# Gate and up products on separate halves of TensorE's rows, and both block turns in the down phase, in a fused long convolution and SwiGLU layer

## The chip, the cores and the metric

The kernel runs on one core of a Trainium2 chip. The metric is the device time of one execution in microseconds (us), the median of several runs. The core has a matrix engine (TensorE, PE in the profile; its weight loads are listed apart as PEld), a vector engine (VectorE, DVE), an activation engine (ScalarE, ACT), a general engine (GpSimd, POOL) and a sync engine (SyncE, SP) whose queue issues nearly all DMAs here. TensorE multiplies a stationary operand of up to 128 rows by 128 columns with a moving operand of up to 512 columns, and writes to PSUM. PSUM is used as four buffers of two banks, 512 float32 values per partition in each bank. SBUF is the working memory of 128 partitions.

## What is computed

A sequence of S = 2048 tokens with D = 576 features goes through two residual halves. The first is a gated long convolution: its causal convolution runs along the sequence, as products of spectra. The second is a feed-forward layer with F = 4608 hidden columns. Both have a layer norm and a modulation by a row that a condition vector gives.

```python
x = A_q
sa, ca, ga, sb, cb, gb = ...                     # six rows of silu(c) @ w_mod
h = layernorm(x) * (1 + ca) + sa
x = x + ga * conv_part(h, A_k, A_v, ...)         # q * (long convolution of (shifted k * v))
h = layernorm(x) * (1 + cb) + sb
gate = h @ w1                                    # 576 -> 4608
up = h @ w3                                      # 576 -> 4608
x = x + gb * ((silu(gate) * up) @ w2)            # 4608 -> 576
```

All inputs are bfloat16; sums are kept in float32.

## The kernel before

The convolution works in eight blocks of 256 tokens (B), the feed-forward layer in four row blocks of 512 tokens (RB), so that a row block holds two convolution blocks. `run` computes block 0 of the convolution first (`first_block`). Then a first stage runs 24 of the 36 hidden tiles of 128 columns for tokens 0 to 255, while the convolution of block 1 is worked off beside it (`conv_second`). Then `row_blocks` runs r = 0 to 3. Row block 0 begins with the two chunks whose weights are still in place, then alternates between the three chunks that are new (all 512 tokens) and the four that need only tokens 256 to 511.

A row block has an up phase (`stream`) and a down phase (`down`). While they run, the convolution of the two blocks of the next row block (`conv`) is worked off a step at a time. It is a Python generator; after each item `advance` pulls so many of its steps as the spent time allows, so its instructions stand between the products on every engine's queue. `outcome` ends a block's convolution: real parts of the accumulated spectrum z, inverse transform, the residual, the second layer norm into `h2row`.

**The turn.** The products need the normed rows with the features on partitions. `turn_all` does that for a block of 256 tokens: ten transposes of 128 columns (five for each of two token groups) into one PSUM buffer, then five evictions on ACT (`turned`, line 601), which also apply scale and shift per feature (`cbcol`, `sbcol`). 576 features are four full tiles of 128 and a rest of 64. So that the rest can serve gate and up at once, its 64 features are written twice into the row (columns 512 to 575 and 576 to 639), and land on partitions 0 to 63 and 64 to 127 of the fifth tile. The turned rows lie in `h2T`, two buffers used in turn by row blocks. The first block is turned by `turn_split` and `turned_split`, on ACT and DVE side by side. The later of a row block's two blocks is turned in the down phase of the row block before (line 985), the earlier one within the convolution, between the residual and the norm of the later (line 856).

**The up phase.** Hidden columns come in nine chunks of four tiles (FC = 4). `load_w13` brings a chunk's columns of w1 and w3 into one of two buffers `wst`, by four DMAs (lines 871 and 872): for each matrix 512 rows as four tiles on 128 partitions (512 KB), and the last 64 rows on partitions 0 to 63 for w1, 64 to 127 for w3 (64 KB). A buffer is loaded again as soon as the products that read it are through. An item is one PSUM buffer: gate in one bank, up in the other, 512 columns each (one hidden tile for 512 tokens, or two for 256). It takes eight full products (`full`, line 916) per hidden tile, and two products of 64 rows for the rest (`rest`, line 927). The latter use different halves of TensorE's rows and run side by side. Items are taken in pairs, or in fours in the last row block: the full products of the early ones, the rests of the early and of the late ones together, then the full products of the late ones. Then `hide` takes silu(gate) and up out of PSUM on ACT and multiplies them on DVE into `h3`.

**The down phase.** For each half h of the 576 output columns, nine chunks of w2 are multiplied (line 979), 16 products of 288 columns for a chunk, four token groups accumulating in two PSUM buffers (four in the last half of all).

Of the kernel before, what the change touches and what calls it, by code (L numbers as in the profile page):

```python
# [9 lines left out]
BF16 = mybir.dt.bfloat16  # L10
F32 = mybir.dt.float32
# [4 lines left out]
P = 128  # L16
S = 2048
D = 576
# [5 lines left out]
RB = 512  # L24
NRB = S // RB
# [9 lines left out]
EPS = 1e-5  # L35

# [7 lines left out]
class _Kernel:  # L44
# [28 lines left out]
    def setup(self):  # L73
# [12 lines left out]
        self.h2T = [const.tile([P, 5, RB], BF16, name=f"h2T{i}") for i in range(2)]  # L86
        self.h2row = const.tile([P, 2, 640], BF16, name="h2row")
# [5 lines left out]
        self.cbcol = const.tile([P, 5], F32, name="cbcol")  # L93
        self.sbcol = const.tile([P, 5], F32, name="sbcol")
# [23 lines left out]
        nc.gpsimd.memset(self.h2T[0][:, 0, :], 0.0)  # L118
# [117 lines left out]
    def mod_columns(self):  # L236
# [13 lines left out]
        nc.scalar.activation(self.cbcol[:], ps[:, 0, 0:5], ACT.Copy, bias=1.0)  # L250
        nc.scalar.copy(self.sbcol[:], ps[:, 1, 0:5])
# [298 lines left out]
    def residual(self, s, y):  # L550
        nc = self.nc
        x1, hg = self.xo[s], self.hg[s]
        nc.vector.tensor_mul(hg[:], hg[:], y[:])
        nc.vector.tensor_add(x1[:], x1[:], hg[:])

    def normed(self, s, cc, m, r):

        row, x1 = self.h2row, self.xo[s]
        self.center(row[:, cc, 0:D], x1[:, cc, :], m, r)
        self.center(row[:, cc, D:640], x1[:, cc, 512:D], m, r)  # L560

    def normed_act(self, s, r, b):
        row, x1 = self.h2row, self.xo[s]
# [5 lines left out]
    def turn(self, pt, cc):  # L569
        for ct in range(5):  # L570
            self.nc.tensor.transpose(pt[:, cc, ct * P:(ct + 1) * P],  # L571
                                     self.h2row[:, cc, ct * P:(ct + 1) * P], self.ident[:])

    def turn_split(self, cc):

        pt = [self.ps((P, 2, 1024), BF16) for _ in range(2)]
        for ct in range(5):
            self.nc.tensor.transpose(pt[ct // 3][:, 0, ct % 3 * P:(ct % 3 + 1) * P],
                                     self.h2row[:, cc, ct * P:(ct + 1) * P], self.ident[:])
        return pt  # L580

    def turned_split(self, pt, cc):
        hT = self.h2T[0]
        for ct in range(5):
            dst, src = hT[:, ct, cc * P:(cc + 1) * P], pt[ct // 3][:, 0, ct % 3 * P:(ct % 3 + 1) * P]
            if ct > 2:
                self.nc.vector.tensor_scalar(dst, src, self.cbcol[:, ct:ct + 1], self.sbcol[:, ct:ct + 1],
                                             op0=ALU.mult, op1=ALU.add)
            else:
                self.nc.scalar.activation(dst, src, ACT.Identity, bias=self.sbcol[:, ct:ct + 1],  # L590
                                          scale=self.cbcol[:, ct:ct + 1])

    def turned(self, s, pt, c0, n):

        nc = self.nc
        hT = self.h2T[(s // 2) % 2]
        t = 2 * (s % 2) + c0
        for ct in range(5):
            dst = hT[:, ct, t * P:(t + n) * P].rearrange("p (c t) -> p c t", c=n)
            src = pt[:, c0:c0 + n, ct * P:(ct + 1) * P]  # L600
            nc.scalar.activation(dst, src, ACT.Identity, bias=self.sbcol[:, ct:ct + 1],  # L601
                                 scale=self.cbcol[:, ct:ct + 1])
# [25 lines left out]
    def first_block(self):  # L628
# [18 lines left out]
        self.warm(3, self.h2T[0][:, 0, :])  # L647
# [3 lines left out]
        self.warm(4, self.h2T[0][:, 0, :])  # L651
# [84 lines left out]
    def outcome(self, s, fill, waits, between=None, quick=False):  # L736


        def steps():
# [3 lines left out]
            y = self.lnp.tile([P, 2, D], BF16, name="y", tag="y")  # L743
# [25 lines left out]

    def turn_all(self, s):  # L770

        pt = self.ps((P, 2, 1024), BF16)
        for cc in range(2):
            self.turn(pt, cc)
        self.turned(s, pt, 0, 2)
# [20 lines left out]
    def conv(self, s0):  # L796
# [59 lines left out]
        yield from self.outcome(s1, ahead, (5.0, 4.5, 5.0, 0.0), lambda: self.turn_all(s0))  # L856
# [7 lines left out]
    def load_w13(self, fc):  # L864
# [5 lines left out]
        for i, w in enumerate((self.w1, self.w3)):  # L870
            nc.sync.dma_start(t[:, 5 * i:5 * i + 4, :], w[0:512, cols].rearrange("(a p) f -> p a f", p=P))
            nc.sync.dma_start(t[64 * i:64 * i + 64, 4, :], w[512:D, cols])
# [12 lines left out]
    def stream(self, r, jobs, rate, size):  # L885

        nc = self.nc
        hT = self.h2T[r % 2]
        items = []
        for job in jobs:
            m = RB // (job[2] - job[1])
            items += [(job, fi, m) for fi in range(0, FC, m)]
        gus, ws = {}, {}

        def load(job):
# [7 lines left out]
            ws[job[0:3]] = w  # L907


        def full(k, first):  # L910
            (fc, t0, t1, _, _), fi, m = items[k]
            w, n = ws[fc, t0, t1], t1 - t0
            for a in range(m):
                for i in range(2):
                    for ct in range(4):
                        nc.tensor.matmul(gus[k][:, i, a * n:(a + 1) * n],  # L916
                                         w[:, 5 * i + ct, (fi + a) * P:(fi + a + 1) * P], hT[:, ct, t0:t1],
                                         start=(first and ct == 0 and a == 0),
                                         stop=(not first and ct == 3 and a == m - 1))

        def rest(k, first):
            (fc, t0, t1, _, _), fi, m = items[k]
            w, n = ws[fc, t0, t1], t1 - t0
            for a in range(m):
                for i in range(2):
                    rows = slice(64 * i, 64 * i + 64)
                    nc.tensor.matmul(gus[k][:, i, a * n:(a + 1) * n],  # L927
                                     w[rows, 4, (fi + a) * P:(fi + a + 1) * P], hT[rows, 4, t0:t1],
                                     start=(first and a == 0), stop=(not first and a == m - 1))

        def hide(k):
            (fc, t0, t1, _, _), fi, m = items[k]
            sg = self.hp.tile([P, RB], BF16, name="sg", tag="sg")
            nc.scalar.activation(sg[:], gus[k][:, 0, :], ACT.Silu)  # L934
            u = self.hp.tile([P, RB], BF16, name="u", tag="u")
            nc.scalar.copy(u[:], gus[k][:, 1, :])  # L936
            f = fc * FC + fi
            nc.vector.tensor_mul(self.h3[:, f:f + m, t0:t1], sg[:].rearrange("p (a t) -> p a t", a=m),  # L938
                                 u[:].rearrange("p (a t) -> p a t", a=m))
            del gus[k]  # L940
            self.advance(rate * 2.05)

        def begin(k):
            if items[k][1] == 0:
                load(items[k][0])
            gus[k] = self.ps()
        for k in range(0, len(items), size):
            early, late = range(k, k + size // 2), range(k + size // 2, k + size)
            for m in early:
                begin(m)  # L950
                full(m, True)
            for m in early:
                rest(m, False)
            for m in late:
                begin(m)
                rest(m, True)
            for m in early:
                hide(m)
            for m in late:
                full(m, False)  # L960
                hide(m)

    def down(self, r, rate):
        nc = self.nc
        for h in range(2):
# [4 lines left out]
            for f0 in range(0, NF, W2C):  # L970
# [11 lines left out]
                if h == 1 and f0 // W2C == 5 and r + 1 < NRB:  # L982

                    self.end()
                    self.turn_all(2 * r + 3)
                if (f0 // W2C) % 4 == 3:
# [118 lines left out]
```

## Time and profile before

| What | us |
|---|---|
| median of 3 runs | 523.21 (521.06 to 523.32) |
| profiled execution, its own time | 520.12 |
| span of that profile (first to last instruction) | 518.3 |
| mean granted TensorE clock | 0.992 |
| PE busy | 499.9 (96% of the span), 3362 products |
| PEld busy | 293.8 (57%) |
| DVE busy | 341.0 (66%) |
| ACT busy | 293.3 (57%) |
| POOL busy | 54.9 (11%) |
| full products of the up phase, line 916 | 267.4 busy, x1344 |
| 64-row products, line 927 | 43.2 busy, x336 |
| down products, line 979 | 145.6 busy, x1152 |
| DMA queue of SP | 107.21 MB, 64.3% of 16 engines |

The page lists each engine's busy time, then a chain of waits: the work that ended last, followed back from the end. Only time on that chain sets the span. The timeline lists one engine's instructions in order, merged into groups: start, length to the end of the last one, the group and its count. A group's length runs past the start of the next one by the depth of the pipeline, so distances between starts are what counts. Views of stretches give each engine's busy time between two moments, and in the last three columns the granted clock, the share of time in which the 16 DMA engines were busy, and the GB/s that they moved.

In time the program falls into these parts: block 0 of the convolution to about 33 us; the first stage to 70.7; row block 0 to 171.4; row block 1 to 291.0; row block 2 to 407.3; row block 3 to the end.

### The profile page before, as it was taken

To read this page: it belongs to the slowest core of one execution; us is meant where nothing else is said; L and a number is where in the kernel's file an instruction comes from. 1 tells how busy PE (TensorE), PEld (TensorE's weight loads), DVE (VectorE), ACT (ScalarE), POOL (GpSimd) and SP (SyncE) were. 2 spreads that over 40 slices of the span, in tenths; PEclk is the share of its full clock that TensorE was granted. 3 is DMA by queue.
4 is the path that set the end of the run, shared out by engine and by line. 5 is a ranking of instruction groups with operands and counts; after the bars stand their busy time and mean duration, and the time that the engine had idled before them with its cause. 6 is when DMAs were issued, how large, how long until landed. Compare 5 with 4: busy or idle time off the path is not lost.

```text
span 518.3 us, 8731 instructions
## 1 busy us (share of the span) xinstructions
PE 499.9 (96%) x3362; PEld 293.8 (57%) x3362; DVE 341.0 (66%) x515; ACT 293.3 (57%) x581; POOL 54.9 (11%) x109
## 2 busy tenths in 40 slices
PE   7999988999999999999998999999999999999997
PEld 3666765555788444444676543434588544444775
DVE  8898996999995355896999995389661212222012
ACT  6668469668543469759561465876816446445000
POOL 3205001204021001202002000120101000000000
PEclk9999889999999999999999999999999999999999
DMA  8959629757679953547999894554455453450462
GB/s 269 313 178 332 201 89 321 275 183 250 197 208 348 330 176 107 188 158 275 363 365 352 318 284 150 165 178 156 152 143 145 147 173 119 161 169 10 118 179 70
DMA packets 102205, 107.77 MB, mean 208 GB/s; under 512 B 5075, under 2 KB 94228, under 8 KB 102164
## 3 DMA queue, kind: packets, MB, share of 16 engines
q1 hardware_dynamic: 102142, 107.21, 64.3%
q8 instruction: 26, 0.43, 0.3%
q14 instruction: 15, 0.12, 0.1%
q10 hardware_dynamic: 22, 0.01, 0.0%
HBM read 96.00 MB, written 11.21 MB: 207 GB/s over the span
## 4 chain that ended last, share of the span: by engine, by line
PE 84%; DMA 8%; ACT 4%; DVE 2%; issue 1%; POOL 1%; DVEq 0%
PE ps L916 46%; PE ps L979 25%; PE ps L927 7%; DMA wst<-in_B_w_dram 5%; DMA w2t<-in_B_w_dram 3%; PE ps L313 2%; PE ps L539 2%; PE ps L364 1%; PE ps L299 1%; ACT junk L440 1%; PE ps L571 1%; PE ps L219 0%; PE ps L626 0%; ACT sg L934 0%; DMA shk_raw<-in_A_shift_k_dram 0%
## 5 line engine op out<-in xcount | busy, mean ns | idle before, releaser
L916 PE MATMUL ps<-h2T,wst 128*128 128x512 bf16 (+1 forms) x1344 | 267.4, 351 | 5.9 <-DMA wst<-in_B_w_dram 3.0
L916 PEld LDWEIGHTS <-wst 128*128 128x128 bf16 x1344 | 128.1, 98 | 128.6 <-issue 19.7
L934 ACT ACTIVATE sg<-ps 128x512 bf16<-128x512 f32 x144 | 86.6, 601 | 117.0 <-PE ps L927 73.9
L979 PE MATMUL ps<-w2t,h 128*128 128x288 bf16 x1152 | 145.6, 286 | 3.1 <-DMA w2t<-in_B_w_dram 2.3
L979 PEld LDWEIGHTS <-h 128*128 128x128 bf16 x1152 | 112.2, 98 | 32.5 <-issue 4.0
L938 DVE TENSOR_TENSOR h<-sg,u 128x512 bf16<-128x512 bf16 x144 | 60.5, 422 | 96.6 <-ACT u L936 96.6
L936 ACT CAST u<-ps 128x512 bf16<-128x512 f32 x144 | 84.5, 587 | 0.2 <-DVE h L938 0.2
L410 DVE TENSOR_TENSOR p<-X,V 128x3456 bf16<-128x3456 bf16 x28 | 54.7, 1953 | 5.1 <-DMA X<-Xd 4.9
L412 DVE TENSOR_TENSOR z<-z,p 128x3456 bf16<-128x3456 bf16 x28 | 54.7, 1954 | 0.2
L997 DVE TENSOR_TENSOR og<-ps,gbrow 128x288 bf16<-128x288 f32 x32 | 13.2, 450 | 48.9 <-PE ps L979 48.9
L927 PE MATMUL ps<-h2T,wst 64*128 64x512 bf16 (+1 forms) x336 | 43.2, 355 | 0.4 <-ACT kT L366 0.4
L440 ACT ACTIVATE junk<-x 128x576 bf16<-128x576 bf16 x54 | 37.5, 695 | 0.5
L601 ACT ACTIVATE h2T<-ps,sbcol,cbcol 128x256 bf16<-128x256 bf16 x35 | 16.7, 569 | 24.8 <-PE ps L571 24.8
L927 PEld LDWEIGHTS <-wst 64*128 64x128 bf16 x336 | 11.6, 95 | 28.1 <-issue 24.1
L455 POOL TENSOR_SCALAR l2m<-l2s 128x2 f32<-128x2 f32 x6 | 8.9, 1476 | 153.3 <-ACT junk L440 153.3
L334 DVE TENSOR_TENSOR kvt<-kh,shk 128x1152 bf16<-128x1152 bf16 x24 | 18.1, 753 | 7.4 <-DMA kh<-in_A_k_dram 7.2
L455 POOL TENSOR_SCALAR l1m<-l1s 128x2 f32<-128x2 f32 x7 | 6.5, 929 | 139.4 <-ACT junk L440 139.4
L566 ACT ACTIVATE h2row<-x,l2n,l2r 128x576 bf16<-128x576 bf16 (+1 forms) x24 | 13.7, 642 | 12.5 <-POOL l2n L460 12.4
L335 DVE TENSOR_TENSOR kv<-kv,kvt 128x1152 bf16<-128x1152 bf16 x24 | 18.1, 753 | 0.3
L315 ACT CAST X<-ps 128x576 bf16<-128x576 f32 x24 | 15.5, 658 | 0.0
L405 DVE TENSOR_TENSOR z<-X,V 128x3456 bf16<-128x3456 bf16 x7 | 13.7, 1953 | 2.5 <-DMA X<-Xd 2.5
L745 ACT CAST y<-ps 128x576 bf16<-128x576 f32 x14 | 8.4, 651 | 10.2 <-PE ps L539 10.2
(137 smaller groups left out, 356.3 us busy)
## 6 DMA issues: line engine op xcount, KB each, us to landing
wst<-in_B_w_dram SPq DMA_DIRECT2D x80, 512.0 KB, 4.5
w2t<-in_B_w_dram SPq DMA_DIRECT2D x72, 288.0 KB, 3.2
X<-Xd SPq DMA_DIRECT2D x8, 864.0 KB, 5.8
Xd<-X SPq DMA_DIRECT2D x6, 864.0 KB, 6.4
wst<-in_B_w_dram SPq DMA_DIRECT2D x80, 64.0 KB, 2.2
kh<-in_A_k_dram SPq DMA_DIRECT2D x7, 720.0 KB, 6.9
Vd<-V SPq DMA_DIRECT2D x4, 864.0 KB, 6.3
V<-Vd SPq DMA_DIRECT2D x4, 864.0 KB, 5.0
```

The source lines that it names most:

```text
L334: nc.vector.tensor_mul(tmp[:], kh[:, 3 - j:5 - j, :], tap(j))
L335: nc.vector.tensor_add(kv[:], kv[:], tmp[:])
L410: nc.vector.tensor_mul(p[:], X[:], V[:])
L412: nc.vector.tensor_add(z[:], z[:], p[:])
L440: self.nc.scalar.activation(junk[:], src[:, i, :], func, accum_out=out[:, col:col + 1])
L601: nc.scalar.activation(dst, src, ACT.Identity, bias=self.sbcol[:, ct:ct + 1], scale=self.cbcol[:, ct:ct + 1])
L916: nc.tensor.matmul(gus[k][:, i, a * n:(a + 1) * n], w[:, 5 * i + ct, (fi + a) * P:(fi + a + 1) * P], hT[:, ct, t0:t1], start=(first and ct ...
L927: nc.tensor.matmul(gus[k][:, i, a * n:(a + 1) * n], w[rows, 4, (fi + a) * P:(fi + a + 1) * P], hT[rows, 4, t0:t1], start=(first and a == 0 ...
L934: nc.scalar.activation(sg[:], gus[k][:, 0, :], ACT.Silu)
L936: nc.scalar.copy(u[:], gus[k][:, 1, :])
L938: nc.vector.tensor_mul(self.h3[:, f:f + m, t0:t1], sg[:].rearrange("p (a t) -> p a t", a=m), u[:].rearrange("p (a t) -> p a t", a=m))
L979: nc.tensor.matmul(acc[t], self.h3[:, f0 + f, t * P:(t + 1) * P], w[:, f, :], start=(f0 + f == 0), stop=(f0 + f == NF - 1))
```

## The change

The contraction over 576 features is cut into nine pieces of 64 (NK). All gate products run on TensorE's rows 0 to 63 and all up products on rows 64 to 127, each pair at once. A hidden tile of 512 tokens takes 18 products of 64 rows where it took eight of 128 and two of 64. `h2T` holds nine turned tiles; tile j has features 64j to 64j + 63 on its lower half and the next 64 on its upper half, so that with tile j gate uses piece j and up piece j + 1. Pairs run in the order FIRST_J = (0, 5, 1, 6, 2, 7, 3, 8, 4). There is no pairing of items any more, one follows the other.

w1's chunk lies on partitions 0 to 63 of `wst` and w3's on 64 to 127, in nine pieces each, so `load_w13` issues two DMAs of 576 KB, to 64 partitions each, in place of four.

Tile j = 8 takes columns 512 to 639 of the normed row, whose last 64 are a copy of columns 512 to 575 as before; the up product meets that copy with the first 64 rows of w3. So up takes its last piece where the reference has its first; this changes no instruction's kind or size.

```diff
-            nc.sync.dma_start(t[:, 5 * i:5 * i + 4, :], w[0:512, cols].rearrange("(a p) f -> p a f", p=P))
-            nc.sync.dma_start(t[64 * i:64 * i + 64, 4, :], w[512:D, cols])
+            nc.sync.dma_start(t[64 * i:64 * i + 64, :, :], w[:, cols].rearrange("(a p) f -> p a f", p=64))
...
+        def products(gu, w, fi, m, t0, t1):
+            n = t1 - t0
             for a in range(m):
...
+                cols = slice((fi + a) * P, (fi + a + 1) * P)
+                for i, j in enumerate(FIRST_J):
+                    for half in range(2):
+                        rows = slice(64 * half, 64 * half + 64)
+                        nc.tensor.matmul(gu[:, half, a * n:(a + 1) * n], w[rows, (j + half) % NK, cols],
+                                         self.h2T[rows, j, t0:t1], start=(i == 0 and a == 0),
+                                         stop=(i == NK - 1 and a == m - 1))
...
+        for job in jobs:
+            fc, t0, t1 = job[0:3]
+            w, m = load(job), RB // (t1 - t0)
+            for fi in range(0, FC, m):
+                gu = self.ps()
+                products(gu, w, fi, m, t0, t1)
+                hide(gu, fc * FC + fi, m, t0, t1)
+                self.advance(rate * 2.05)
```

A turn now has nine transposes per token group (18 for a block) into two PSUM buffers, and nine evictions. Both turns for the next row block stand in the down phase, the earlier block's after the fourth chunk of the first half. There are two buffers of `h2row` and one of `h2T` (there were one and two). The per-feature scale and shift come as nine columns (`cscol`); every second is put together by two small copies on POOL that move 64 partitions to the other half.

```diff
+    def turn_all(self, s):
+
+        pts = [self.ps((P, 2, 1024), BF16) for _ in range(2)]
+        at = lambda j: slice(j % 5 * P, (j % 5 + 1) * P)
+        t = B * (s % 2)
+        for i, pt in enumerate(pts):
+            js = range(5 * i, min(5 * i + 5, NK))
+            for j in js:
+                for cc in range(2):
+                    self.turn(s, cc, j, pt[:, cc, at(j)])
+            for j in js:
+                self.turned(j, self.h2T[:, j, t:t + B].rearrange("p (c t) -> p c t", c=2), pt[:, :, at(j)])
...
+                if h == 0 and f0 // W2C == 3 and r + 1 < NRB:
+                    self.turn_all(2 * r + 2)
...
-        yield from self.outcome(s1, ahead, (5.0, 4.5, 5.0, 0.0), lambda: self.turn_all(s0))
+        yield from self.outcome(s1, ahead, (5.0, 4.5, 5.0, 0.0))
...
+        nc.scalar.activation(cs[:, 0, 0:10:2], ps[:, 0, 0:5], ACT.Copy, bias=1.0)
+        nc.scalar.copy(cs[:, 1, 0:10:2], ps[:, 1, 0:5])
+        nc.gpsimd.tensor_copy(cs[0:64, :, 1:9:2], cs[64:P, :, 0:8:2])
+        nc.gpsimd.tensor_copy(cs[64:P, :, 1:9:2], cs[0:64, :, 2:10:2])
```

In `turned_split` the first block's nine tiles per token group go five to ACT and four to DVE (three and two before), in the order FIRST_J. The output `y` of the inverse transform no longer has a tile of its own but is written into two rows of z that are free by then.

```diff
-            y = self.lnp.tile([P, 2, D], BF16, name="y", tag="y")
+            z = self.accs[s]
+            y = z[:, 2:6:3, :] if s < SPLIT else z[:, 4:6, :]
```

## The prediction

> **What bounds the kernel now.** I read the page's chain of waits first, then TensorE's (PE's) timeline, the chain cut into pieces, and last the stretches that show the DMA engines.
>
> ```profile
> PE 84%; DMA 8%; ACT 4%; DVE 2%; issue 1%; POOL 1%; DVEq 0%
> ```
>
> TensorE sets the end: 84% of the chain. Its timeline, in the second and the last row block (start, length, group):
>
> ```profile
> 213.18 3.63 PE L916 MATMUL ps<-h2T,wst 128*128 128x512 bf16 x16
> 216.74 0.60 PE L927 MATMUL ps<-h2T,wst 64*128 64x512 bf16 x4
> 217.28 3.63 PE L916 MATMUL ps<-h2T,wst 128*128 128x512 bf16 x16
> ...
> 427.75 7.08 PE L916 MATMUL ps<-h2T,wst 128*128 128x512 bf16 x32
> 434.76 1.04 PE L927 MATMUL ps<-h2T,wst 64*128 64x512 bf16 x8
> 435.73 7.08 PE L916 MATMUL ps<-h2T,wst 128*128 128x512 bf16 x32
> ```
>
> Two items take 217.28 - 213.18 = 4.10 us, four take 435.73 - 427.75 = 7.98 us, each with one excursion to 64-row products. An item is nine slots (eight full products and a side-by-side pair): 18a + T = 4.10 and 36a + T = 7.98 give a slot of a = 0.216 us and T = 0.22 us for one excursion, out and back. Eight 64-row products fill 0.97 us, four slots and a way in: a pair costs one slot. With 256 columns eight fill 0.54 us, 0.11 a pair.
>
> The 8% of DMA is what matters here. The same chain, its DMA pieces before 131 us:
>
> ```profile
> 44.54 8.16 DMA wst<-in_B_w_dram
> ...
> 79.11 7.37 DMA wst<-in_B_w_dram
> ...
> 94.55 5.47 DMA wst<-in_B_w_dram
> ...
> 121.89 5.67 DMA wst<-in_B_w_dram
> ```
>
> In these four places weight loads already set the pace: wst has two buffers, and a load may start only when the job before last has ended.
>
> And what a load to 64 partitions does. By queue order, the 1728 KB of the first w_mod piece (128 partitions) run from about 7 us to 12.4, then its 216 KB on partitions 0 to 63, then 1152 KB on 128 again. Stretches (the last two columns are the DMA engines' busy share and GB/s):
>
> ```profile
> 12.00:12.50 0.50, 0.50 (x6) 0.39 (x4) 0.50 (x2) 0.50 (x2) 0.00 (x0) 1.00 1.00 392
> 12.50:13.00 0.50, 0.50 (x7) 0.22 (x4) 0.50 (x2) 0.50 (x2) 0.00 (x0) 1.00 1.00 217
> 13.00:13.50 0.50, 0.50 (x7) 0.33 (x5) 0.43 (x4) 0.50 (x3) 0.00 (x0) 1.00 0.93 247
> ...
> 14.75:15.75 1.00, 0.61 (x5) 0.25 (x3) 1.00 (x3) 1.00 (x3) 0.80 (x2) 1.00 1.04 411
> ```
>
> The engines are just as busy, and move little more than half. [...]
>
> **Part 1, excursions.** After the change products never leave the 64-row form on their own; an excursion is left wherever other work of TensorE stands between two items, and once on entering a row block from the down phase. Counting groups in the timeline: before, 6 in the first stage and 12, 18, 18, 9 in the row blocks, 63. After: 7, 11 + 1, 14 + 1, 12 + 1 and 1, 48. So 15 x 0.22 = **-3.3 us**. The slots stay nine an item. That pairs run on at one slot is shown for four in a row; for 18 narrow ones in a row the nearest sustained row is the sixty one-column products, 3.66 us from 23.23 to 26.89, 61 ns with their weight load. Two such per slot are 0.122 against 0.11, over 432 narrow slots 0 to +5.2 us; I take 0, since pairs themselves show 0.11.
>
> **Part 2, turns.** A turn of a block has 18 transposes for 10, seven times; ten take 0.56 us (146.27 to 146.83): 56 x 0.056 = **+3.1 us**. Nine evictions for five on ACT, four more at 0.57 us: in the down phases hidden behind down products (from 164.47 nine take 5.1 us, the next row block starts at 171.43); without that cover 2.3 us a turn. The second PSUM buffer per turn leaves none free in the down phase for up to three microseconds; later convolution bursts are few there, so 0, at most 2 us a turn. The turn that ends the first stage has no cover:
>
> ```profile
> 70.10 2.40 ACT L601 ACTIVATE h2T<-ps,sbcol,cbcol 128x256 bf16<-128x256 bf16 x5
> ```
>
> Evictions follow each other by 0.45 us and products wait for each. The eighth pair needs the ninth eviction, done about 70.1 + 9 x 0.45 = 74.2, where nine slots would have been through at 72.7 before: **+1.7 us**. The block turned at the very start has ten ACT evictions for six at 0.37 us (six take 2.20); the first item ends 0.6 us later: **+0.6 us**. The two column moves on POOL (0.55 and 0.66 us are its nearest rows) lie before 30.00, when DVE asks for its scales; uncovered 1.2 us. Moving the earlier block's turn from the convolution into the down phase puts ten plus eight transposes on PE's queue in front of down products, which wait if the normed rows are late; these are written some 20 us earlier, so 0. y in z costs nothing: the same copies, and z is next written two blocks later.
>
> **Part 3, loads.** Four DMAs a chunk (512, 64, 512, 64 KB) become two of 576 KB, each on 64 partitions: 1.18 MB. At 354 GB/s, the rate from 424.5 to 426.8, they took 3.3 us; at 217, 5.4 us. A 64 KB load lands after 2.2 us, 1.9 of it fixed. So a load takes 1.9 + 5.4 = 7.3 us from its release. It is also needed whole at once, where before the gate's 512 KB sufficed to begin.
> - In a row block of full jobs the window is four items, 36 x 0.216 = 7.8 us and more: it just fits, 0. One load there shares the queue with a spill of 864 KB (2.5 us): about +1.6.
> - In row block 0 half-width jobs stand between, windows 4 to 6 us (a job's first and last full product are found by counting 32 a job along PE's timeline). Chunk 6: landed 86.5 (79.11 + 7.37) + 2.1, begun at 85.02, less 0.5 waited already, +3.1. Chunk 7: released 94.14, so 101.5 for 98.50, less 0.5, +2.5. Chunk 8: 107.19, 114.5 for 113.02, +1.5. Chunk 3: 121.48, 128.8 for 125.91, less 1.1, +1.8. Together +8.9.
> - First stage: two loads 2.1 longer in the stretch of the 8.16 us piece, less 0.9 waited there: +3.3.
> - From 250 to 291 the DMA engines are full (shares 1.07 and 1.02), and two loads lie there: +4.2 of DMA time, of which I take half, +2.1.
>
> Sum **+15.9 us**. With the 288 GB/s of the fastest half microsecond of that mixed stretch (14.0 to 14.5) a load takes 6.0 and the sum is some 6; with half of 354 it takes 8.6, full windows fail too (0.3 to 0.8 each of some twenty), and it is some 39. I take 217, the stretch that holds most of such packets. The saving of two issues a chunk on SP (about 0.5 us each) is worth nothing where the load's transfer is the wait.
>
> [...]
>
> **Sum.** -3.3 + 3.1 + 1.7 + 0.6 + 15.9 = +18 us on the profiled execution, 520.12 us (span 518.3). The runs shown have a median of 523.21, so the forecast is **541 us**.
>
> **Rivals.**
> - *Faster: two large loads land sooner than four.* Place: the four DMA pieces above. With 576 KB to 64 partitions at 354 GB/s and half the issues on SP, the waits for wst go (3.0 us of PE, some 4 more as weight loads): -3.3 + 5.4 - 7 = -5, 518 us. It decides if a 576 KB load in the last row block lands within 3.9 us. For it: there 512 KB take 3.6. Against: the stretches. 0.12.
> - *The loads cost little*: the two halves overlap in the queue and part 3 comes to 0 to +2, the rest staying +2: 523 to 527 us. Against: one queue, in order. 0.10, of which 0.07 within 0.5%.
> - *Issue is the limit on narrow pairs*, on top of the forecast: 546 us. 0.08.
> - *The halves don't run side by side*: nine more slots an item, 144 x 1.94 = +280 us. The 0.97 us for eight rules it out: 0.02.
> - *DMA-bound throughout*, the 39: 564 us. 0.08.
>
> **How the numbers follow.** The forecast has 0.6. Low: the loads at 288 GB/s and a little more hidden, 524; high: near the case of full windows failing, 560. Beyond lie the faster case and part of the last, under 2 in 10. 0.5%, 2.6 us, is what can be told from no change: faster 0.12, within 0.07, slower 0.81.
>
> **What would show it.** Matmul groups of 64 rows throughout the up phase, nine pairs in 1.94 us; 48 excursions of 0.22; a landing of 576 KB after some 4.6 us and the second 2.7 later; PE waiting for wst some 20 us in all, mostly from 40 to 131 us; a last row block (407 to 479 before) about 1.8 us shorter. A last row block longer than before, or pairs slower than 0.216, would say that the price of a slot is wrong; no longer landing, that the loads are.

## The result and the profile after

The changed kernel takes 587.37 us (median of 4 runs, 585.44 to 589.4), the kernel before 522.13 beside it: a ratio of 1.125, 95% interval 1.1194 to 1.1306. The forecast was 541, the range 524 to 560. The direction was right, the size was not: 65 us where 18 had been worked out.

The page of the changed kernel: busy time, the granted clock by slices, the chain of waits, the groups that matter, and the loads with their median time to landing.

```profile
span 587.6 us, 11433 instructions
PE 522.0 (89%) x4769; PEld 311.4 (53%) x4770; DVE 347.6 (59%) x519; ACT 308.6 (53%) x613; POOL 47.1 (8%) x111
PEclk9889798879999999999997998999799999999999
PE 43%; DVE 24%; DMA 16%; ACT 12%; issue 3%; POOL 1%; SPq 0%; ACTq 0%; DVEq 0%
L903 PE MATMUL ps<-h2T,wst 64*128 64x512 bf16 (+1 forms) x3024 | 308.6, 358 | 29.9 <-DMA wst<-in_B_w_dram 21.6
wst<-in_B_w_dram SPq DMA_DIRECT2D x80, 576.0 KB, 7.0
```

TensorE's share of the chain has fallen from 84% to 43%, and DVE's has risen from 2% to 24%, though DVE does nearly the same work (347.6 us busy against 341.0). PE's busy time is 22.1 us longer (522.0 against 499.9) and its idle time 47.2 us (65.6 against 18.4); together that is the 69.3 us by which the span grew. The longer busy time is hardly more work, since the slots are the same and by the forecast's own terms the added transposes (+3.1) and the saved excursions (-3.3) cancel: the mean granted clock fell from 0.992 to 0.955, and an estimate from it, 587.6 x 0.045 - 518.3 x 0.008, gives 22.3 us.

Where PE waits, and where ACT does: first two views of the changed kernel, then the same lines of the kernel before (total us, times, longest).

```profile
PE ps L903 <- DMA wst<-in_B_w_dram: 21.6, 11, 3.9
PE ps L543 <- ACT u L911: 8.3, 4, 3.1
PE ps L940 <- DMA w2t<-in_B_w_dram: 6.4, 2, 5.9
PE ps L903 <- ACT u L911: 5.0, 7, 2.0
```

```profile
ACT sg L909 <- DVE h L912: 67.9, 27, 4.3
```

```profile
PE ps L916 <- DMA wst<-in_B_w_dram: 3.0, 4, 1.1
PE ps L979 <- DMA w2t<-in_B_w_dram: 2.3, 3, 1.1
```

```profile
ACT sg L934 <- DVE h L938: 7.4, 6, 1.7
```

The 21.6 us on weight loads are what the forecast had named (some 20). But there is a second wait that it had not: ACT stands 67.9 us for DVE's product h, where it stood 7.4, and PE then for a PSUM buffer that ACT hasn't emptied. DVE's timeline in row block 2 shows why. First the changed kernel (start, length, group):

```profile
404.14 0.42 DVE L912 TENSOR_TENSOR h<-sg,u 128x512 bf16<-128x512 bf16 x1
404.48 1.95 DVE L414 TENSOR_TENSOR p<-X,V 128x3456 bf16<-128x3456 bf16 x1
406.35 0.75 DVE L339 TENSOR_TENSOR kv<-kv,kvt 128x1152 bf16<-128x1152 bf16 x1
407.01 1.95 DVE L416 TENSOR_TENSOR z<-z,p 128x3456 bf16<-128x3456 bf16 x1
408.88 0.42 DVE L912 TENSOR_TENSOR h<-sg,u 128x512 bf16<-128x512 bf16 x1
...
411.89 0.41 DVE L912 TENSOR_TENSOR h<-sg,u 128x512 bf16<-128x512 bf16 x1
412.23 0.75 DVE L530 TENSOR_TENSOR z<-z 128x1152 bf16<-128x1152 bf16 x1
412.90 1.95 DVE L414 TENSOR_TENSOR p<-X,V 128x3456 bf16<-128x3456 bf16 x1
414.88 1.96 DVE L416 TENSOR_TENSOR z<-z,p 128x3456 bf16<-128x3456 bf16 x1
416.75 0.42 DVE L912 TENSOR_TENSOR h<-sg,u 128x512 bf16<-128x512 bf16 x1
```

Then the same work in the kernel before:

```profile
345.66 0.42 DVE L938 TENSOR_TENSOR h<-sg,u 128x512 bf16<-128x512 bf16 x1
346.00 1.95 DVE L410 TENSOR_TENSOR p<-X,V 128x3456 bf16<-128x3456 bf16 x1
347.87 0.41 DVE L938 TENSOR_TENSOR h<-sg,u 128x512 bf16<-128x512 bf16 x1
348.20 1.95 DVE L412 TENSOR_TENSOR z<-z,p 128x3456 bf16<-128x3456 bf16 x1
350.07 0.41 DVE L938 TENSOR_TENSOR h<-sg,u 128x512 bf16<-128x512 bf16 x1
```

Before, one long operation of the convolution stands between two products h, and h comes every 2.2 us, an item's time. After, two or three stand there (1.95 + 0.75 + 1.95 = 4.65 us), and h comes up to 4.9 us apart while PE could end an item every 1.95 (the 36 items of run 8's last row block take 70.1). sg and u have two buffers each; when they are full ACT stops, PSUM isn't emptied, and PE stops (timeline of PE, with the idle time ahead of a group and what ended it):

```profile
413.53 2.12 PE L903 MATMUL ps<-h2T,wst 64*128 64x512 bf16 x18 [0.56 <-ACT u L911]
418.39 1.09 PE L543 MATMUL ps<-z,Fb 128*128 128x288 bf16 x4 [2.74 <-ACT u L911]
422.59 1.12 PE L543 MATMUL ps<-z,Fb 128*128 128x288 bf16 x4 [3.11 <-ACT u L911]
423.64 3.60 PE L903 MATMUL ps<-h2T,wst 64*128 64x512 bf16 x16
```

The last line shows what followed these waits: 16 of an item's 18 narrow products take 3.60 us (all 18 take 4.02), where the 18 of the first line take 2.12. From 418.5 to 428.5 us the granted clock was 0.50. The stretches 410 to 424 and 424 to 437 us have a granted clock of 0.80 and 0.82.

No line of the diff reorders DVE's work on the convolution. The kernel's instructions are put in order by a planner before the run, engine by engine, and that order changed. Matched by the tiles that they read and write, 427 of DVE's 515 operations still follow each other as in the kernel before, and 523 of ACT's 538 (leaving out the turns); SP's transfers moved too.

### The profile page after: what moved, and what is told of

The parts are those of the page before. It is cut to its first block, busy times and chain, and to the rows that moved or that the text cites. A ratio compares the mean times of both kernels' runs of the same rounds, so it can differ in the third digit from the quotient of the medians.

```text
span 587.6 us, 11433 instructions
## 1 busy us (share of the span) xinstructions
PE 522.0 (89%) x4769; PEld 311.4 (53%) x4770; DVE 347.6 (59%) x519; ACT 308.6 (53%) x613; POOL 47.1 (8%) x111
## 4 chain that ended last, share of the span: by engine, by line
PE 43%; DVE 24%; DMA 16%; ACT 12%; issue 3%; POOL 1%; SPq 0%; ACTq 0%; DVEq 0%
PE ps L903 22%; PE ps L940 16%; DMA wst<-in_B_w_dram 6%; DVE p L414 6%; DVE z L416 5%; DMA w2t<-in_B_w_dram 3%; ACT junk L444 3%; ACT sg L909 3%; ACT u L911 2%; DMA knat<-in_A_ssm_k_dram 2%; DVE h L912 2%; DVE kvt L338 2%; DMA kh<-in_A_k_dram 2%; DVE kv L339 2%; DMA X<-Xd 1%
## 5 line engine op out<-in xcount | busy, mean ns | idle before, releaser
L903 PE MATMUL ps<-h2T,wst 64*128 64x512 bf16 (+1 forms) x3024 | 308.6, 358 | 29.9 <-DMA wst<-in_B_w_dram 21.6
L903 PEld LDWEIGHTS <-wst 64*128 64x128 bf16 x3024 | 153.5, 97 | 175.7 <-DMA wst<-in_B_w_dram 29.8
L940 PEld LDWEIGHTS <-h 128*128 128x128 bf16 x1152 | 112.6, 98 | 39.6 <-issue 10.2
L581 ACT ACTIVATE h2T<-ps,cscol 128x256 bf16<-128x256 bf16 (+1 forms) x73 | 33.0, 565 | 36.1 <-PE ps L574 36.1
L543 PE MATMUL ps<-z,Fb 128*128 128x288 bf16 x80 | 12.9, 307 | 8.3 <-ACT u L911 8.3
L459 POOL TENSOR_SCALAR l2m<-l2s 128x2 f32<-128x2 f32 x6 | 4.4, 740 | 191.1 <-ACT junk L444 191.1
L570 ACT ACTIVATE h2row<-x,l2n,l2r 128x576 bf16<-128x576 bf16 (+1 forms) x24 | 13.8, 652 | 9.7 <-POOL l2n L464 9.7
L557 DVE TENSOR_TENSOR hg<-hg,z 128x1152 bf16<-128x1152 bf16 x7 | 5.3, 759 | 17.3 <-ACT z L750 17.3
L543 PEld LDWEIGHTS <-Fb 128*128 128x128 bf16 x80 | 8.1, 103 | 12.5 <-issue 10.0
```

Source lines behind the costliest of these rows:

```text
L543: nc.tensor.matmul(ps[:, h, 0:H], self.Fb[:, b, cs], z[:, row, h * H:(h + 1) * H], start=(i == 0), stop=(i == len(terms) - 1))
L581: self.nc.scalar.activation(dst, src, ACT.Identity, bias=bias, scale=scale)
L903: nc.tensor.matmul(gu[:, half, a * n:(a + 1) * n], w[rows, (j + half) % NK, cols], self.h2T[rows, j, t0:t1], start=(i == 0 and a == 0), st ...
L940: nc.tensor.matmul(acc[t], self.h3[:, f0 + f, t * P:(t + 1) * P], w[:, f, :], start=(f0 + f == 0), stop=(f0 + f == NF - 1))
```

## The experiments

Two theories stood at the start. LOADS: the two loads to 64 partitions are the loss, by PE's waits for wst and by X, kh and V that land late beside them. ORDER: the new order on DVE is.

**Runs 1 to 4: the loads and the order, one at a time.** The loads of before in the changed kernel (run 1), DVE held to the order in which the program issues its work (run 2), both (run 3), and the loads of the change in the kernel before (run 4).

```diff
-            nc.sync.dma_start(t[64 * i:64 * i + 64, :, :], w[:, cols].rearrange("(a p) f -> p a f", p=64))
+            nc.sync.dma_start(t[:, 5 * i:5 * i + 4, :], w[0:512, cols].rearrange("(a p) f -> p a f", p=P))
+            nc.sync.dma_start(t[64 * i:64 * i + 64, 4, :], w[512:D, cols])
...
+        since = len(self.nc.cur_bb.bb.instructions)
...
+        self.in_order(since, [self.nc.vector.engine])
```

> The changed kernel with the four weight loads of before (128 partitions; the weights then lie in other places than the products read them, so gate and up products use wrong weight rows; number, size and time of the products are as in the changed kernel). Theory LOADS (the 64-partition loads hold PE, and slow X, kh and V beside them; nothing else costs much): 520 to 528 us, with DVE's conv work between two h products still as in the changed kernel or not, without effect. Theory ORDER (DVE and ACT get their convolution work in lumps twice as long between two items, so sg, u and PSUM come free late): 570 to 587 us, the waits of ACT on h stay near 68 us and only PE's 22 us on wst go partly. Both: 545 to 565 us.

> The changed kernel with DVE held to the order in which the program issues its work, in the first stage and the row blocks; loads as in the changed kernel. LOADS: 580 to 590 us, unchanged. ORDER: 525 to 550 us (about the first forecast, 541, if the loads cost what was forecast), the waits of ACT on h fall from 68 us to under 15. Both: 545 to 570 us.

> The changed kernel with the loads of before (weights then lie in other places than the products read) and DVE in program order. If LOADS and ORDER together are the whole loss: 515 to 528 us, near the kernel before. If something third costs (the transposes, the narrow products' issue, ACT's evictions): 535 us or more.

> The kernel before with the two 576 KB loads of the change (its products then read weights that lie in other places). It prices the loads alone, under before's order of DVE and ACT. LOADS as the main loss: 560 to 585 us. The first forecast's price of the loads (+16): 535 to 545 us. ORDER alone: 522 to 530 us.

| run | us | ratio to before (521.36) |
|---|---|---|
| 1 changed, loads of before | 579.49 | 1.1115 (1.0945 to 1.1285) |
| 2 changed, DVE in program order | 599.74 | 1.1503 (1.1372 to 1.1635) |
| 3 both | 580.75 | 1.1139 (1.1075 to 1.1204) |
| 4 before, loads of the change | 559.62 | 1.0734 (1.0648 to 1.082) |

The loads alone cost 38 us in the kernel before, and yet giving them back gains only some 8 in the changed one (run 1's two executions took 575.76 and 583.21). So neither theory holds alone, and the two losses hide behind each other. Run 1 still has the new wait in full:

```profile
ACT sg L910 <- DVE h L913: 79.7, 32, 4.5
```

Runs 2 and 3 miss the times that ORDER expected, although ACT's waits for h do fall, to 12.3 and 17.1 us. Program order isn't the order of before either: in run 3 it puts 1.5 to 4.2 us between nearly all products h, so that DVE is busy 76.6 us in the 90.2 of row block 1's up phase (54.6 of 78.2 before) and idles in the down phase (15.1 of 46.9). The convolution's kv then comes late, and PE, on whose queue its transforms stand between the products, waits for it (run 3; 21.4 us in run 2):

```profile
PE ps L317 <- DVE kv L341: 22.3, 6, 7.2
```

The test had to be the order of before itself.

**Runs 5 to 7: the order of before on DVE.** The order in which DVE's convolution operations and products h stand in the kernel before was carried over: each convolution operation is held behind the h that it follows there. Run 5 has the loads of before as well, run 6 those of the change. Run 7 is the kernel before with each h held behind the convolution operations that stand ahead of it in the changed kernel.

```diff
+AFTER_H = (
+    (3921, 3952, 3953),
...
+    def after_h(self):
+        by = {i.name: i for i in self.nc.cur_bb.bb.instructions}
+        for h, *rest in AFTER_H:
+            for i in rest:
+                self.tc.add_manual_dep(
+                    by[f"I-{i}"], f"I-{h}",
+                    mybir.DependencyInfo(mybir.DependencyClass.NoSync, mybir.DependencyReason.DATA),
+                    reason="planned order")
```

> The changed kernel with the loads of before (weights then lie in other places than the products read), and on DVE each convolution operation held behind the h product that it follows in the kernel before, so that DVE has 1.5 to 2.7 us of such work between two h products in the row blocks' up phases where the changed kernel has up to 5.4. ORDER (the planner's order on DVE is what costs, beside the loads): 515 to 530 us, ACT's waits on h under 15 us. STRUCTURE (the narrow pairs themselves, or items begun one at a time and not by twos, cost, whatever the order on DVE): 560 to 580 us, as with the loads of before alone (579.5).

> The changed kernel with its own loads, on DVE each convolution operation held behind the h product that it follows in the kernel before. What is over 522 is then the price of the loads in this kernel. ORDER: 550 to 562 us, close to the kernel before with the loads of the change (559.6), some us less for the excursions that are gone. STRUCTURE: 580 to 595 us.

> The kernel before, its loads and products untouched, with DVE held to the changed kernel's order: each h product behind the convolution operations that stand ahead of it there. ORDER: 555 to 580 us, with ACT's waits on h at 40 us or more (7.4 in the kernel before). STRUCTURE: 520 to 532 us.

Measured: 547.81 us (ratio 1.0487, 1.0442 to 1.0531), 571.69 (1.0948, 1.0882 to 1.1014) and 546.12 (1.0458, 1.0399 to 1.0517), before 522.53. The order on DVE is a cause, shown from both sides: giving it back takes 31.7 us off run 1 (79.7 us of ACT's waits become 29.7) and 15.7 off the changed kernel, where the order on SP and, leaving out the turns, on ACT stayed as it was, and laying the changed kernel's order on the kernel before costs 24. But all three are between the two theories' numbers; run 5 stands 25 us over before. Its largest single wait is this:

```profile
PE ps L1026 <- DMA w2t<-in_B_w_dram: 6.9, 1, 6.9
```

The issues on SP's queue about that time (start, length):

```profile
268.85 0.33 SPq L522 DMA_DIRECT2D X<-Xd  x1
269.28 0.47 SPq L955 DMA_DIRECT2D wst<-in_B_w_dram  x1
...
272.04 0.54 SPq L954 DMA_DIRECT2D wst<-in_B_w_dram  x1
272.63 0.50 SPq L366 DMA_DIRECT2D knat<-in_A_ssm_k_dram  x1
...
273.81 4.92 SPq L1019 DMA_DIRECT2D w2t<-in_B_w_dram  x4
```

The down phase, which reads w2t, had begun at 263.42, so the first w2t loads of this phase were issued 10.4 us behind its start. In the kernel before it begins at 249.65, and the first w2t loads stand in the queue 3.7 us behind that and ahead of the last wst pieces:

```profile
253.32 1.38 SPq L972 DMA_DIRECT2D w2t<-in_B_w_dram  x2
...
257.32 1.02 SPq L872 DMA_DIRECT2D wst<-in_B_w_dram  x1
```

SP's order had changed too.

**Runs 8 to 11: the order of before on SP as well.** In the row blocks SP's transfers follow each other as in the kernel before, and DVE's order is held as in runs 5 and 6. Run 8 has the loads of before, run 9 those of the change, run 10 those of the change cut into four, run 11 is the kernel before with the loads of the change and its own order held.

```diff
+        for late, early in PLANNED:
+            self.tc.add_manual_dep(
+                by[f"I-{late}"], f"I-{early}",
...
-        for i, w in enumerate((self.w1, self.w3)):
-            nc.sync.dma_start(t[64 * i:64 * i + 64, :, :], w[:, cols].rearrange("(a p) f -> p a f", p=64))
+        for lo, hi in ((0, 5), (5, NK)):
+            for i, w in enumerate((self.w1, self.w3)):
+                nc.sync.dma_start(t[64 * i:64 * i + 64, lo:hi, :],
+                                  w[64 * lo:64 * hi, cols].rearrange("(a p) f -> p a f", p=64))
```

> As the changed kernel with before's loads and DVE order (547.8 us; weights lie in other places than the products read), and in addition SP's transfers in the row blocks held to the order in which the kernel before issues them. QUEUE (the rest of the loss is SP's order: in the second row block w2t is issued only 10 us after the down phase could start, behind X loads, and wst late in row block 0): 518 to 532 us, the 6.9 us wait on w2t at 280 us gone. PAIRS (items one at a time, 18 transposes, the new products): 543 to 550 us.

> The changed kernel with its own loads, DVE and SP held to the order of the kernel before (each pair of loads where before's tail loads stand). What is left over 522 is the price of the loads and of the products. If the first forecast's sum was right for an unchanged order: 535 to 548 us. If the loads cost what they cost in the kernel before (38): 555 to 565 us.

> As the run before it, with each pair of 576 KB loads cut into four by rows and issued in turn (gate rows, up rows, gate rows, up rows), so that transfers to the lower and to the upper 64 partitions stand next to each other in the queue. If two halves move side by side when both are under way: 10 us or more less than the run before it. If the transfers stay one after the other: within 4 us of it.

> The kernel before with the two 576 KB loads of the change (its products then read weights that lie in other places) and DVE and SP held to the order of the kernel before. If the 38 us of these loads were in part the planner's new order: 535 to 550 us. If they are the transfers themselves: 555 to 562 us.

Measured: 541.08 us (1.0362, 1.0327 to 1.0397), 560.77 (1.076, 1.0696 to 1.0824), 559.39 (1.0712, 1.0682 to 1.0741) and 556.73 (1.0664, 1.0581 to 1.0747), before 521.91. SP's order is worth 6.7 us with the loads of before (547.8 to 541.1) and 10.9 with the new ones (571.7 to 560.8). With the order settled the loads cost 560.8 - 541.1 = 19.7 us here, and 556.7 - 521.9 = 34.8 in the kernel before (38 where its order was free). PE's waits for wst, run 8 and then run 9:

```profile
PE ps L990 <- DMA wst<-in_B_w_dram: 14.2, 10, 4.1
```

```profile
PE ps L978 <- DMA wst<-in_B_w_dram: 23.5, 12, 4.4
```

QUEUE held for the wait at 280 us, now under 2 us, but not for the whole: run 8 is still 19 us over before. Stage by stage, in us of the profiles, from the first product of a phase to the first of the next:

| stage | before | after | run 1 | run 5 | run 8 | run 9 |
|---|---|---|---|---|---|---|
| first stage and row block 0, up | 99.2 | 128.1 | 117.1 | 110.8 | 113.5 | 130.3 |
| row block 0, down | 39.5 | 43.3 | 46.0 | 40.0 | 40.0 | 40.3 |
| row block 1, up | 78.2 | 85.6 | 86.4 | 78.8 | 78.9 | 78.4 |
| row block 1, down | 41.3 | 51.0 | 50.6 | 50.1 | 46.5 | 47.3 |
| row block 2, up | 78.3 | 93.3 | 91.3 | 80.6 | 77.2 | 81.0 |
| row block 2, down | 38.0 | 39.7 | 39.6 | 40.4 | 40.4 | 40.4 |
| row block 3, up | 71.9 | 71.0 | 70.0 | 70.2 | 70.1 | 71.8 |

The profile of run 9 is that of its longest execution, 566.64 us. Run 8 matches before from row block 1's up phase on, but for the down phase of row block 1, where the DMA engines are full (share 1.05 before), and the one after it. Fourteen of its us lie in the first stage and row block 0, where even the loads of before are waited for (12.9 us of its 14.2). A possible reason, tested in runs 13 and 14: before, the rows of gate were wanted first and let go first, with up's and the rest's behind them; a pair wants both halves of a tile at once and lets both go at its end. Run 10 said nothing on the two halves, since the order held was that of pieces in the kernel before, and put the four pieces as up, up, gate, gate.

**Runs 12 to 15: alternating halves, tile borders, excursions.** Run 12 issues the four pieces gate, up, gate, up. Runs 13 and 14 leave out the four re-reads of weights in row block 0 (in the kernel before, and in run 8's kernel, there with the order of run 13 held). Run 15 takes items by fours in the kernel before from row block 1 on.

```diff
-                again = [(fc, 256, 512, None, None) for fc in range(n1 - 2)]
+                again = [(fc, 256, 512, "last", None) for fc in range(n1 - 2)]
...
+            if w == "last":
+                w = self.last
...
-            self.stream(r, jobs, rate, 4 if r == NRB - 1 else 2)
+            self.stream(r, jobs, rate, 4 if r > 0 else 2)
```

> The changed kernel with each pair of 576 KB loads cut into four and issued gate rows, up rows, gate rows, up rows (the earlier cut stood up, up, gate, gate in the queue, since the order held was that of the pieces of before), DVE and SP otherwise in the order of the kernel before. If two transfers to different halves of the partitions move side by side when they stand next to each other: 541 to 550 us, and the share of the DMA engines in the last row block falls from 0.59 towards 0.43. If not: 556 to 562 us and 0.59.

> The kernel before without the four re-reads of weights in row block 0 (the products of these jobs read the tile loaded last, so that part of the output is computed with other weights). The control for the next run: 510 to 522 us; the few waits on wst that it had there (2 to 4 us) go.

> The changed kernel with before's loads, DVE and SP in the order of the run beside it, and without the four re-reads in row block 0 (those products read the tile loaded last; the others read rows in other places). With the re-reads this stood 19 us over the kernel before, 14 of it in the first stage and row block 0. BORDER (pairs need gate and up rows of a tile at once and free them at its end, so a load has less time between release and need, and row block 0 reads a tile for every 4 us of products): 3 to 10 us over the run beside it. PAIRS (the products or their evictions cost there): 14 us or more over it.

> The kernel before with items taken by fours from the second row block on, not in the last one alone: 18 excursions between 64-row and 128-row products less at some 0.2 us each. If the evictions and the convolution's products still find a free PSUM buffer: 517 to 520 us. If four items hold PSUM too long: 525 us or more.

Measured, before 522.05: run 12 551.69 us (1.057, 1.0528 to 1.0613), run 13 523.97 (1.004, 1.0019 to 1.0062), run 14 537.78 (1.0333, 1.0269 to 1.0397), run 15 525.44 (1.0068, 1.0032 to 1.0103).

- Run 12 is 9 us faster than run 9, between its two expectations. By the profiles, of which run 9's is a long one, 8.8 us lie in the first stage and row block 0 (121.5 us for 130.3). The reason given isn't borne out: in the last row block the DMA engines' share is 0.57 at 129 GB/s (run 9: 0.59 at 131; with the loads of before in run 8 0.43 at 134), and the 1152 KB of a tile with next to nothing beside it still take 5.7 to 6.3 us from first packet to last (run 9: 5.7 to 6.9), so two halves don't move side by side there. Why the order of the pieces matters where other transfers run beside them stays open.
- Runs 13 and 14: without the re-reads the difference is 13.8 us, where it was 19.2. So some 5.4 us, give or take 4 by the intervals, are the tile borders in row block 0; BORDER had expected 3 to 10 to be left, and 13.8 is nearly the 14 of PAIRS. The kernel before gains nothing without its re-reads: they were covered. The other 13.8 us are spread (by the profiles 2.4 before the first stage, 5.7 from there to the end of row block 0's up phase, 2.5 in each of the next two down phases and 2.4 in the third, small ones of either sign), and I can't name one cause for them. Three things are known of them: each down phase now has 36 transposes for 20, by the forecast's 0.056 us an estimated 0.9 us; PE still waits 9.2 us for wst (4.4 in run 13); and ACT's order was never given back, it is in run 14 what it is in the changed kernel.
- Run 15 removes 18 excursions and is 0.7% slower: the up phases of row blocks 1 and 2 take 81.4 and 80.4 us for 78.2 and 78.3. PE waits 5.1 us for ACT ahead of the convolution's products there, a wait that isn't among those of 0.7 us and more in the kernel before. There are four PSUM buffers, and four items hold them all.

**Runs 16 and 17: why the order changed.** The up products are left out and ACT reads gate's sums twice; run 17 has the loads of before. No order is held.

```diff
-                    for half in range(2):
+                    for half in range(1):
...
-            nc.scalar.copy(u[:], gu[:, 1, :])
+            nc.scalar.copy(u[:], gu[:, 0, :])
```

> The changed kernel without its up products: nine 64-row products an item where it has nine pairs; ACT reads the gate's sums twice (the output leaves out up). No order is held. On the chip a single narrow product takes a slot as a pair does, so TensorE's time per item stays near 1.95 us. PLANNER (it orders DVE, ACT and SP as if the two products of a pair came one after the other, an item twice as long, and so halving their number undoes the new order): DVE's lumps between two h products fall back to 1.5 to 2.7 us and the time to 550 to 570 us, like the changed kernel with the order of before held (560.8 with DVE and SP). If the order has another source (the loads, the turn, items one at a time): 582 to 592 us, lumps as in the changed kernel.

> The same with the loads of before (the gate's weights then lie in other places than the products read; up is left out). PLANNER: 533 to 550 us, like the 541.1 with the order of before held. Another source: 570 to 582 us, as with the loads of before alone (579.5).

Measured: 633.93 us (four runs from 611.83 to 650.16, at mean clocks of 0.81 to 0.85) and 569.45 (1.0846, 1.0747 to 1.0944; clock 0.894). The times miss both theories. The clock shows as a reason: in run 17 it was 0.50 in every stretch read from 80 to 180 us (see the end), and run 16's mean clocks are below run 17's. The stages behind that stretch, where the clock was 1.00 again (185 to 190 us), say more: in run 17 row block 1 takes 77.5 and 42.8 us, row block 2 77.0 and 38.4, where run 1, the same but for the second product of each pair, has 86.4 and 50.6, 91.3 and 39.6. In these stages ACT waits 51.1 us for h in run 1; in the whole of run 17 it waits this long:

```profile
ACT sg L910 <- DVE h L913: 2.2, 2, 1.2
```

DVE has again one long operation between two products h there:

```profile
406.55 0.42 DVE L913 TENSOR_TENSOR h<-sg,u 128x512 bf16<-128x512 bf16 x1
406.89 1.96 DVE L414 TENSOR_TENSOR p<-X,V 128x3456 bf16<-128x3456 bf16 x1
408.76 0.42 DVE L913 TENSOR_TENSOR h<-sg,u 128x512 bf16<-128x512 bf16 x1
409.09 1.95 DVE L416 TENSOR_TENSOR z<-z,p 128x3456 bf16<-128x3456 bf16 x1
```

PE's slots per item are the same on the chip in both, as far as items at the same clock show it: nine single products of run 17 take 4.02 us at 0.50 (from 105.85), and so do the nine pairs of the changed kernel (from 423.64). Only the number of products that the planner sees is halved, and the long stretches between products h are gone, though the order isn't wholly that of before (450 of DVE's 515 operations follow each other as there, 427 in run 1). So the planner seems to set the other engines' work against a TensorE that does the two products of a pair one after the other. That it counts so is inferred from this pair of runs; its reckoning itself is not shown. Nor are the pairs the only thing that it reacts to: in run 4, the kernel before with the loads of the change, three stretches of DVE work between two products h in row block 2's up phase are 3.9 to 4.7 us long, where the longest was 2.7, and ACT waits 18.5 us for h in all (7.4 before).

**The account.** From 587.4: DVE's order -15.7 (run 6), SP's order -10.9 (run 9), the loads -19.7 (run 8), and 19.2 left to the 521.9 of before, 5.4 of them at the borders of re-read tiles. By the intervals each is good to some 4 us. The sizes hold for this sequence: the loads would be some 8 if taken first. No version ran faster than the kernel before; the fastest form of the change with its own loads is run 12, 551.69.

## Why the prediction was wrong, point by point

- *Nine pairs in 1.94 us, no slot added:* right. The timeline has 18 narrow products in 2.12 us with the pipeline's depth, and with undisturbed loads the last row block is 1.8 us shorter (run 8: 70.1 for 71.85), as forecast; in the changed kernel 0.9.
- *Excursions -3.3:* right in size as far as the last row block shows it. Run 15 adds that such a gain can be lost again to waits for a PSUM buffer, 5.1 us there.
- *Turns +3.1 and +1.7, start +0.6:* small, as forecast. PE's wait on the turned rows, over the whole kernel, is 2.2 us (1.6 before). The move of the earlier block's turn was none on the chip: before, both turns stood in the down phase already, 20 transposes in each, and now 36. The start took 3.6 us more in the changed kernel, but from 0.1 to 3.2 more in runs 5, 6, 8 and 9, which have the same code there but for the loads in two of them, so its 0.6 can't be read.
- *The loads, +15.9:* that loads to 64 partitions take longer was right and the size near, 19.7 in the changed structure once the order was that of before. A lone tile's 1152 KB moved at 209 GB/s at best, over the whole tile, where 217 was taken, the first load of a tile landed in the last row block after 5.3 to 5.7 us where 4.6 was named (the rival of faster loads needed 3.9), and PE waited 21.6 us for wst where some 20 were named. What the term lacked is the clock: behind PE's waits of 2.74 and 3.88 us in the lines shown here it was 0.50 for 10.0 and 3.3 us (418.5 to 428.5, with another wait of 3.11 in it, and 104.5 to 107.8). Over the whole kernel the lower clock is the estimated 22 us, beside 47 of idle time; some 3 of them, by an estimate from 26 to 32 us at 0.50, have no such wait ahead (the last idle time before them, 0.45 us, ends at 22.96). The rival with full windows failing had 39 for the loads; in the kernel before they do cost 34.8 to 38, though no run shows the half of 354 that it was worked out from: 209 is 0.59 of it.
- *"Sum. -3.3 + 3.1 + 1.7 + 0.6 + 15.9":* this is the step that failed. It priced each edit in the timeline of before, as if all other work kept its place. The order of DVE's and SP's work is worked out anew for each program, and a pair that takes one slot on the chip seems to weigh as two products there. 26.6 us (15.7 + 10.9) come from the order, and no term or rival held any of it. Of the 47.5 us between the 18 of the forecast and the 65.5 measured, these are the largest part; 3.8 are the loads, and 17.1 (19.2 less the forecast's other 2.1) have no cause shown but the 5.4 of the tile borders. The description ahead of the forecast has the convolution's instructions stand between the products as the program pulls them; the planner's part is missing there. "No pairing of items any more" had no price either, and some of the last 13.8 us may be its own.
- *The saving of issues on SP is worth nothing:* not tested by itself; nothing in the runs speaks against it.

## What to carry to other kernels

Where a planner or list scheduler sets the order of the engines, a change of form that adds no slot on the chip (nine pairs in 1.95 us here) can still move work on engines that it never touches: compare the order on each engine, and the longest stretch between two evictions, before pricing anything else. When two losses overlap, undoing one shows little (some 8 us here) and adding it to the old kernel shows much (38); do both before naming a share. Count a wait of TensorE with any slower products behind it: here 3.88 us of idle time had 35 products in 5.74 us behind them, 1.9 more than at 1.94 for 18.

## What was not expected of the hardware

The clock after a wait. In run 17 PE idled some 2 us in all between 75 and 79 us and ran little but transposes beside, and the granted clock (last column but two) then fell to 0.50 and stood there to the down phase, with PE busy for all of the time from 81 to 180 us (whether the waits or the transposes lowered it isn't shown):

```profile
75.00:77.00 2.00, 1.48 (x24) 1.16 (x21) 1.97 (x4) 2.00 (x6) 0.00 (x0) 1.00 0.20 62
79.00:81.00 2.00, 1.99 (x10) 1.19 (x10) 1.97 (x2) 2.00 (x4) 0.00 (x0) 0.53 0.51 119
110.00:130.00 20.00, 20.00 (x66) 9.45 (x65) 13.40 (x18) 5.82 (x11) 0.00 (x0) 0.50 0.53 161
175.00:180.00 5.00, 5.00 (x26) 3.41 (x25) 1.76 (x3) 1.07 (x2) 0.00 (x0) 0.50 0.60 177
180.00:185.00 5.00, 5.00 (x28) 3.36 (x27) 3.25 (x4) 2.19 (x3) 0.00 (x0) 0.51 0.59 176
```

Through a hundred microseconds of single products on 64 rows, with a few full ones between, it stayed at 0.50; under the full down products, which begin at 181.58, it came back (1.00 from 185 to 190). Under pairs on both halves it came back too. PE in the changed kernel:

```profile
103.87 5.74 PE L903 MATMUL ps<-h2T,wst 64*128 64x512 bf16 x35 [3.88 <-DMA wst<-in_B_w_dram]
109.55 0.42 PE L317 MATMUL ps<-kv,Fb 128*128 128x288 bf16 x2
109.90 2.12 PE L903 MATMUL ps<-h2T,wst 64*128 64x512 bf16 x18
```

After the wait the 35 narrow products take 5.7 us, 1.9 more than at 1.94 us for 18; the clock is 0.50 from 104.5 to 107.8 us and 1.00 from 108 on. Behind the wait that ends at 422.59 it took longer: 0.50 to 428.5 us, 1.00 from 428.75. In run 17 PE was busy for all of the 20 us from 110 to 130 at 0.50, so being busy didn't bring the clock back there. Whether the rows in use decide it isn't shown: only runs 16 and 17 have an up phase of single products, and nothing was varied between 64 and 128 rows.
